# A transformer block with adaptive LayerNorm: normalisations on GpSimd in another form, x of the first chunk earlier, a shorter warm-up and a new order of work

## The chip, the cores and the metric

The kernel runs on one NeuronCore of a Trainium2 chip. The metric is the device time of one execution in microseconds (us); the kernel before takes 338.66 us, the median of three runs between 338.33 and 340.01. The five engines have separate instruction streams: PE is TensorE (matrix products; PEld is its weight load), DVE is VectorE, ACT is ScalarE, POOL is GpSimd, and SP is SyncE, which here only issues transfers. Each works through its instructions in the order in which they were emitted, and waits at semaphores for the others.

## What is computed

One transformer block on a sequence of 2048 tokens with 640 features, batch 1. A modulation vector `silu(c) @ w_mod` gives six vectors of 640, which scale, shift and gate the two halves of the block. Attention has 32 heads of 20 features, each token looking at the 256 tokens up to itself; the MLP has 1536 hidden features. Cut to what matters:

```python
mod = (silu(c) @ w_mod).reshape(1, 6, 1, -1)        # sa, ca, ga, sb, cb, gb
h = layernorm(x) * (1 + ca) + sa
q, k, v = split(h @ wqkv)                           # 32 heads of 20
p = softmax(where(0 <= i - j < 256, q k^T / sqrt(20), -1e9))
x = x + ga * ((p v) @ wo)
h = layernorm(x) * (1 + cb) + sb
x = x + gb * ((sigmoid(h @ w_gate) * (h @ w_up)) @ w_down)
```

The function `layernorm` has no weights of its own: `(x - m) / sqrt(v + 1e-5)` over the 640 features. All inputs and the output are bf16.

## The kernel before

The sequence is cut into eight chunks of 256 tokens, each of two blocks of 128 tokens. For every chunk the kernel does the same work: load x, LayerNorm, transpose and modulate (tile hT), project to queries, keys and values, bring queries and keys into the layout QT and KT, compute scores in sets of 2048 columns (PSUM tile S), exp on ScalarE into the tile E, mask E on GpSimd, multiply by V, divide by the sums (the softmax's denominators come out of the same product), send the result through DRAM into the tile oT, multiply by wo, add x, second LayerNorm, transpose and modulate (h2T), MLP, add, store.

The order is not written out by hand. Every instruction is handed to a planner as an operation with the engines that may run it, an expected duration on each, the tiles that it reads and writes, a latency after its end (`lat`) and a priority. The method `schedule` then plays the program through: on each engine it takes, of the operations that could start first (within `PE_EPS` on TensorE), the one with the lowest priority number, and so fixes order, buffer slots and, where several engines may do the work, the engine. A table `PRI` adds a number to the priority of every kind of operation of every chunk. `emit` writes the instructions in that order, with the semaphore waits that follow from the tiles. Transfers have an expected share of the bandwidth (`work`) in the plan. So the table and the expected durations set what waits behind what on the chip, although they change no instruction.

What the change touches:

- **LayerNorm** (`ln_stats`, L731 on). VectorE computes statistics (L741, two halves of 320 for each block) and aggregates them (L743); GpSimd adds the epsilon (L746) and takes the power -1/2 (L748) for both blocks at once; then each block is normalised by a `tensor_scalar` over 128 x 640 (L751), which subtracts the mean and multiplies by the power, on VectorE or on GpSimd as the planner decides. The planner expects 0.44 us on VectorE and 0.95 us on GpSimd. Chunks 0 and 1 are then transposed on TensorE against an identity, and scaled and shifted on the way out of PSUM (L786, L787); chunks 2 to 7, and all second LayerNorms, are transposed by SyncE's DMA (L757) and modulated in place (L765 on ScalarE, L766 on VectorE or GpSimd).
- **Masks** (L932, L934). They stand in the same GpSimd stream as the normalisations, and the product of E and V waits for all masks of its sets.
- **The head.** ScalarE's queue issues c and the two x blocks of chunk 0; SyncE's queue begins with five pieces of w_mod (into the memory of wd), then wq and wk in halves, x of chunk 1, wv, the other parts of w_mod (into the memory of wu and hh), wo. VectorE makes c_col and siluc and then silubc, silu(c) copied 128 times (L630). TensorE runs 18 warm-up matmuls of 512 columns on zeros (`warm`, L639), and single filling ones (`fill`, L650) between the pieces of the modulation product (psA, written S<-silubc,wd), whose result is copied to mA (L729) and used at L786 and L787. Two filling matmuls follow the fourth transpose of chunk 0.
- **Bulk loads.** A bulk transfer waits until the one `DEEP` places before it has landed: three are under way at most.

Nearly all matrix products are emitted by one helper and carry line 658 (659 where the array is divided, for the scores and for the product with V), so they are told apart by their tiles: M<-wq,hT is a query projection, M<-h2T,wg the MLP's gate, M<-E,V the product with V.

Of the kernel before, what the change touches and what calls it, by code (L numbers as in the profile page):

```python
# [8 lines left out]
ALU = mybir.AluOpType  # L9
# [8 lines left out]
NDT = D // 128  # L18
# [376 lines left out]
def c_pe(n):  # L395
# [3 lines left out]
PE_EPS = 0.117  # L399
PRI = {  # L400
    "amodu2": 349.1, "amodu3": 69.8, "amodu4": -2, "amodu5": 20.4, "amodu6": 21.9, "amodu7": 33.4, "apow0": -17.1,
    "apow1": -0.2, "apow2": -233.1, "apow3": -9.4, "apow4": -4.7, "apow5": -39.6, "apow6": -201.2, "apow7": 26.9,
    "astats1": 2, "astats2": -137.3, "astats3": 147.7, "astats4": 52, "astats5": 202.7, "astats6": 112.2,
    "astats7": -8.8, "atr3": -6.2, "atr4": -3.2, "atr5": -194.6, "atr6": 10.3, "atr7": -24.5, "axh0": -203,
    "axh2": -66.7, "axh3": 71.6, "axh4": -24.4, "axh5": 33.9, "axh6": -20.5, "axh7": 9.8, "bmodu0": -166.8,
    "bmodu1": 13.9, "bmodu2": 1.5, "bmodu3": 15.4, "bmodu4": -1.8, "bmodu5": 93.1, "bmodu6": 3.4, "bmodu7": -1.2,
    "bpow0": 4.3, "bpow1": 150.8, "bpow2": -11.8, "bpow3": -188.6, "bpow4": -35, "bpow5": 41.6, "bpow6": -22.5,
    "bpow7": -15.1, "bstats0": 20.1, "bstats1": 21.9, "bstats2": 16.8, "bstats3": 14.9, "bstats4": 25.8,
    "bstats5": -84.4, "bstats6": 22.4, "bstats7": -22.6, "btr0": -39.2, "btr1": -39.3, "btr2": -8.5, "btr3": 35,
    "btr5": -82, "btr6": 4.1, "btr7": -2.4, "bxh0": 24.8, "bxh1": -260.1, "bxh2": -55.1, "bxh3": 34, "bxh4": 72.4,  # L410
    "bxh5": 103.8, "bxh6": 81, "bxh7": 17.1, "divide_0": -16.1, "divide_1": 34.3, "divide_2": -154.9,
    "divide_3": 6.6, "divide_4": 14.8, "divide_5": -19.9, "divide_6": -11.9, "divide_7": 6.6, "down0": -15.1,
    "down1": -21.3, "down2": -20, "down4": 0.4, "down5": 1.9, "down7": 60.2, "evqk0": 16.1, "evqk1": 334.5,
    "evqk2": 27.2, "evqk3": 339.9, "evqk4": -0.3, "evqk5": 4.1, "evqk6": -33, "evqk7": -0.3, "evqt0": -11.6,
    "evqt1": -8.4, "evv0": 41.8, "evv1": 235.3, "evv2": 2.5, "evv3": -5.5, "evv4": -16.9, "evv5": -108.2,
    "evv6": -60.1, "evv7": -59.5, "exp0": -116.1, "exp1": -16.2, "exp2": -46.3, "exp3": 5.9, "exp4": -147.4,
    "exp5": -3.4, "exp6": 1.1, "exp7": -126.7, "glu_0": -1.3, "glu_1": 0.5, "glu_2": 26.7, "glu_3": -19.5,
    "glu_4": -37, "glu_5": -3.6, "glu_6": 8.5, "glu_7": 4.2, "hTe0": -31.6, "hTe1": 34.3, "mask0": 136.2,
    "mask2": -61.4, "mask3": 78.7, "mask4": -36.4, "mask5": -30.5, "mask6": 3.2, "mask7": 94.8, "mlpg0": -25,
    "mlpg1": -24.5, "mlpg2": -24, "mlpu0": -25, "mlpu1": -24.5, "mlpu2": -24, "modb": -25.7, "modc": -22.2,  # L420
    "n_ow_0": -20.3, "n_ow_1": -41.5, "n_ow_2": 44.8, "n_ow_3": 103.9, "n_ow_4": -5.8, "n_ow_5": -19.8,
    "n_ow_6": -1.4, "n_ow_7": 33.8, "oT_0": 17.5, "oT_1": 32.5, "oT_2": 12.6, "oT_3": 76.6, "oT_4": -64.2,
    "oT_5": 13.2, "oT_6": 2.6, "oT_7": 49.3, "out": 7.2, "projk0": -33.4, "projk2": 26.4, "projk3": -3.9,
    "projk4": 15.6, "projk5": 1.5, "projk6": 7.4, "projk7": 4, "projq0": -114.6, "projq2": 45.3, "projq3": -8.2,
    "projq4": 6.1, "projq5": -4, "projq6": 8.5, "projq7": -7.9, "projv0": -43.1, "projv1": 8.7, "projv2": 224.6,
    "projv4": -6, "projv5": 2.7, "projv6": 16.2, "projv7": 10.7, "ptr0": -337.9, "ptr1": -256.9, "pv0": -37.3,
    "pv1": -290.4, "pv2": -37.9, "pv3": -37.1, "pv4": -28.1, "pv5": -70.8, "pv6": -10.1, "pv7": -9.1, "qkt2": 7.9,
    "qkt3": 6.7, "qkt4": 64.8, "qkt5": -12.3, "qkt6": -3.6, "qkt7": -4.9, "qtr0": -154.4, "qtr1": -20.9,
    "recip_1": -1.9, "recip_2": 23.6, "recip_3": -2.4, "recip_4": 28.1, "recip_5": -22.7, "recip_6": 2.1,
    "recip_7": -9.2, "res1_0": -0.2, "res1_1": 5, "res1_2": 55.2, "res1_3": 7.6, "res1_4": 13.1, "res1_5": -5.3,  # L430
    "res1_6": -6.4, "res1_7": 11.2, "res2_0": 6.2, "res2_1": -29.9, "res2_2": -5.9, "res2_3": 1.7, "res2_4": -3.1,
    "res2_5": 40.9, "res2_6": -17.8, "res2_7": 2.6, "score0": -287.1, "score1": -347.7, "score2": -20.2,
    "score3": 1.8, "score4": -13.1, "score5": -50.5, "score6": -2.7, "score7": 11.5, "tanh_0": 29, "tanh_1": 20.7,
    "tanh_2": 23.5, "tanh_3": 22.7, "tanh_4": 26.2, "tanh_6": -2.3, "tanh_7": -20.3, "tr1_0": 19.8, "tr1_1": 6.2,
    "tr1_2": -28.1, "tr1_3": 15.6, "tr1_4": 45.4, "tr1_5": -90.8, "tr1_6": -19.7, "tr1_7": 5.2, "tr2_0": 204.6,
    "tr2_1": 224.6, "tr2_2": -128.4, "tr2_3": 42, "tr2_4": 64.5, "tr2_5": 40.4, "tr2_6": 0.1, "tr2_7": 27.5,
# [745 lines left out]
```

The softmax here doesn't subtract the row's maximum and nothing guards it: scores larger than these inputs give would overflow.

## Time and profile before

| what | value |
|---|---|
| median of three runs | 338.66 us |
| span of the profiled run | 335.3 us |
| exp, ACT L924 | 90 x 1876 ns = 168.9 us |
| masks, POOL L932 and L934 | 174 in 144.5 us |
| power, POOL L748 | 16 x 745 ns |
| normalisation on POOL, L751 | 6 x 2516 ns |
| normalisation on VectorE, L751 | 26 x 664 ns |
| modulation on POOL, L766 | 9 x 621 ns (hT), 8 x 559 ns (h2T) |
| statistics, DVE L741 | 64 x 478 ns |

The duration is the time of one instruction on its engine; it says nothing of whether anyone waits for it. For that one needs the chain of work that ended last, the waits of TensorE, and the busy time of each engine stage by stage. In a line of the timeline the first number is the start, the second the time that the merged instructions took, and the bracket at its end gives how long the engine had been idle before it and what ended that.

### The profile page before, as it was taken

How to read it: one execution, taken by the hardware profiler on the slowest of the kernel's cores; microseconds unless marked ns; L12 is line 12 of the kernel's file. 1: busy time of each engine (PE TensorE's matmuls, PEld its weight loads, DVE VectorE, ACT ScalarE, POOL GpSimd, SP SyncE). 2: the span in 40 equal slices, each digit the busy share in tenths (PEclk: the TensorE clock that was granted, in tenths of full speed). 3: DMA queues.
4: the chain of work that ended last, by engine and by line, in shares of the span. 5: the costliest groups of instructions: out<-in, count | busy, mean ns of one | idle time of the engine just before them, and what ended most of it. 6: DMA issues, size and time to landing. Idle time of an engine off the chain costs nothing.

```text
span 335.3 us, 10119 instructions
## 1 busy us (share of the span) xinstructions
PE 326.0 (97%) x4146; PEld 232.6 (69%) x4146; DVE 222.1 (66%) x441; ACT 229.7 (68%) x220; POOL 183.5 (55%) x255
## 2 busy tenths in 40 slices
PE   8898998999999999999999999999999999999996
PEld 3665555666776677766678666776676788887885
DVE  4597786889898857267996476744768663733332
ACT  1597799769988498777899779997699532230120
POOL 4138999766869685646675557656586610100000
PEclk9999999999999999999999999999999999999999
DMA  7989999696970296026851426100140231101101
GB/s 264 376 267 306 302 289 166 138 174 106 270 175 20 78 156 112 22 64 143 122 110 39 88 78 140 46 2 22 64 94 24 61 96 44 23 18 41 41 0 39
DMA packets 71686, 38.72 MB, mean 115 GB/s; under 512 B 46682, under 2 KB 68442, under 8 KB 71642
## 3 DMA queue, kind: packets, MB, share of 16 engines
q1 hardware_dynamic: 71344, 37.76, 46.3%
q8 instruction: 32, 0.52, 0.7%
q10 hardware_dynamic: 298, 0.33, 0.3%
q14 instruction: 12, 0.10, 0.1%
HBM read 21.96 MB, written 5.24 MB: 81 GB/s over the span
## 4 chain that ended last, share of the span: by engine, by line
PE 82%; POOL 6%; DMA 6%; DVE 2%; issue 2%; ACT 1%; SPq 0%; ACTq 0%; POOLq 0%
PE M L658 68%; PE S L659 8%; PE M L659 6%; DMA x<-in_A_x_dram 3%; POOL E L934 2%; POOL E L932 2%; POOL x L751 1%; DMA wo<-in_A_wo_dram 1%; DMA hh<-in_w_mod_dram 1%; DVE x L751 1%; ACT E L924 1%; POOL st L748 0%; DVE st L741 0%; DVE x L1099 0%; DVE stg L813 0%
## 5 line engine op out<-in xcount | busy, mean ns | idle before, releaser
L924 ACT ACTIVATE E<-S 128x2048 bf16<-128x2048 f32 x90 | 168.9, 1876 | 30.6 <-PE S L659 28.2
L932 POOL TENSOR_SCALAR_AFFINE_SELECT E<-E 128x512 bf16<-128x512 bf16 (+2 forms) x90 | 75.9, 844 | 72.3 <-ACT E L924 68.4
L934 POOL TENSOR_SCALAR_AFFINE_SELECT E<-E 128x512 bf16<-128x512 bf16 (+1 forms) x84 | 68.6, 816 | 0.0
L658 PE MATMUL M<-h2T,wg 128*128 128x256 bf16 x480 | 63.6, 273 | 0.1
L658 PE MATMUL M<-h2T,wu 128*128 128x256 bf16 x480 | 63.1, 273 | 0.0
L1080 DVE SCALAR_TENSOR_TENSOR hh<-sig,M 128x512 bf16<-128x512 f32 x48 | 32.6, 680 | 46.1 <-PE M L658 30.8
L1078 ACT ACTIVATE sig<-M 128x512 f32<-128x512 f32 x48 | 28.5, 594 | 43.9 <-PE M L658 43.9
L658 PE MATMUL M<-wd,hh 128*128 128x320 bf16 (+2 forms) x396 | 55.6, 295 | 0.0
L658 PEld LDWEIGHTS M<-h2T,wg 128*128 128x128 bf16 x480 | 45.0, 98 | 9.6 <-issue 2.7
L658 PEld LDWEIGHTS M<-h2T,wu 128*128 128x128 bf16 x480 | 45.9, 98 | 7.4 <-issue 1.7
L658 PEld LDWEIGHTS M<-wd,hh 128*128 128x128 bf16 x396 | 37.0, 98 | 15.4 <-issue 1.7
L659 PE MATMUL S<-QT,KT 20*128 20x256 bf16 (+1 forms) x960 | 35.9, 245 | 0.4 <-DVE KT L813 0.4
L1099 DVE TENSOR_TENSOR x<-M,x 128x320 bf16<-128x320 f32 (+2 forms) x33 | 15.5, 477 | 22.4 <-PE M L658 22.4
L975 DVE STREAM_TRANSPOSE T<-M 128x512 f32<-128x512 f32 x32 | 21.2, 695 | 13.0 <-PE M L659 13.0
L741 DVE BATCH_NORM_STATS2 st<-x 128x6 f32<-128x320 bf16 x64 | 28.2, 478 | 2.3 <-DMA x<-in_A_x_dram 1.9
L659 PEld LDWEIGHTS S<-QT,KT 20*128 20x128 bf16 x960 | 14.1, 92 | 20.7 <-ACT E L924 16.9
L658 PE MATMUL M<-wk,hT 128*128 128x320 bf16 x160 | 25.9, 300 | 0.0
L658 PE MATMUL M<-wq,hT 128*128 128x320 bf16 x160 | 25.5, 299 | 0.1
L658 PE MATMUL M<-wv,hT 128*128 128x320 bf16 x160 | 25.1, 300 | 0.0
L659 PE MATMUL M<-E,V 128*32 128x256 bf16 (+1 forms) x960 | 22.7, 246 | 2.2 <-POOL E L934 1.5
L658 PE MATMUL M<-wo,oT 128*128 128x320 bf16 x160 | 24.7, 300 | 0.0
L659 PEld LDWEIGHTS M<-E,V 128*32 128x32 bf16 x960 | 20.0, 97 | 6.5 <-POOL E L934 2.7
(76 smaller groups left out, 322.3 us busy)
## 6 DMA issues: line engine op xcount, KB each, us to landing
x<-in_A_x_dram SPq DMA_DIRECT2D x30, 160.0 KB
doc<-On SPq DMA_DIRECT2D x64, 40.0 KB
out_dram<-x SPq DMA_DIRECT2D x15, 160.0 KB
wg<-in_B_w_gate_dram SPq DMA_DIRECT2D x5, 384.0 KB
wu<-in_B_w_up_dram SPq DMA_DIRECT2D x5, 384.0 KB
wd<-in_B_w_down_dram SPq DMA_DIRECT2D x4, 480.0 KB
wd<-in_w_mod_dram SPq DMA_DIRECT2D x5, 320.0 KB
wu<-in_w_mod_dram SPq DMA_DIRECT2D x5, 320.0 KB
```

The costliest lines, as they stand in the source:

```text
L658: return e.matmul(o, l, r, start=st, stop=sp, skip_group_check=True)
L659: return e.matmul(o, l, r, start=st, stop=sp, tile_position=tp, skip_group_check=True)
L741: A("dve", lambda e, g, bi=bi, j=j: e.bn_stats(v(bi * 12 + j * 6, 6), src[bi].ap[:, j * 320:(j + 1) * 320]), 0.48, reads=[src[bi].r()], wr ...
L751: A(XHE, lambda e, g, bi=bi: e.tensor_scalar(dst[bi].ap[:], src[bi].ap[:], v(24 + 2 * bi, 1), v(30 + bi, 1), op0=ALU.subtract, op1=ALU.mul ...
L924: A("act", lambda e, eng: e.activation(E.ap[:], Sp.ap[:], ACT.Exp, scale=SM_SCALE), 1.876, reads=[Sp.r()], writes=[E.r()], prio=3, tag=f"e ...
L932: return e.affine_select(ap, ap, pattern=[[0, ap.shape[1]], [1, 128]], compare_op=ALU.is_ge, fill=0.0, base=0, channel_multiplier=-1)
L934: return e.affine_select(ap, ap, pattern=[[0, ap.shape[1]], [-1, 128]], compare_op=ALU.is_ge, fill=0.0, base=-1, channel_multiplier=1)
L975: A("dve", lambda e, g, h=h: e.transpose(T1.ap[:, 512 * h:512 * h + 512], X[h].ap), 0.694, reads=[X[h].r()], writes=[T1.r(h)], prio=3.5, t ...
L1078: A("act", lambda e, g, pg=pg, sg=sg: e.activation(sg.ap[:], pg.ap[:], ACT.Tanh, scale=0.5), c_act(512), reads=[pg.r()], writes=[sg.r()], ...
L1080: A("dve", lambda e, g, pu=pu, sg=sg, f0=f0: e.scalar_tensor_tensor(out=hh.ap[:, f0:f0 + 2, :], in0=sg.ap[:].rearrange("p (a b) -> p a b", ...
L1099: A("dve", lambda e, g, ps=ps, bi=bi, c0=c0, n=n: e.tensor_tensor(x1[bi].ap[:, c0:c0 + n], ps.ap[:, 0:n], x1[bi].ap[:, c0:c0 + n], op=ALU. ...
```

## The change

The normalisation gets another form wherever GpSimd is among the engines allowed: (x - m) r becomes x r + n with n = -m r. GpSimd computes n for each block as a product over one column, after the power. Thirty-two such products are new; they use two more columns of the statistics tile. The planner's durations for the normalisation become 0.5 us on VectorE and 1.2 us on GpSimd.

The two x blocks of chunk 0 move from ScalarE's queue, behind c, to the front of SyncE's queue. The warm-up falls from nine operations of two matmuls to five, and the filling ones between the pieces of the modulation grow from one matmul to two. The copy silubc is made in two halves: the first 64 columns, which the modulation of chunk 0 and the other column products need, and the rest, which only the gates need.

The planner is fed with other landing times of transfers (a `lat` of its own for x, w_mod, the weights and the transposes) and slightly other durations, allows four bulk transfers in place of three, and has a new table of priorities. The new table replaces every number, so it is left out here: with it the order of work changes on all engines, over the whole program.

```diff
-PE_EPS = 0.117
+PE_EPS = 0.141
 PRI = {
...
-DEEP = 3
+DEEP = 4
...
-PACE0 = -95.83
-PACE = 0.103
+PACE0 = 80.17
+PACE = -6.665
...
-FILL = 1
+FILL = 2
...
-        dma(lambda: t.ap[:], lambda: x_flat[b * 128:(b + 1) * 128, :], 0.47 if b > 1 else 0.9, writes=[t.r()], prio=prio, tmin=tmin, tag=f"x{b}" if pool is p_x0 else f"y{b}",
-            eng=eng, lat=0.05 if b > 1 else 1.2)
+        dma(lambda: t.ap[:], lambda: x_flat[b * 128:(b + 1) * 128, :], 0.47, writes=[t.r()], prio=prio, tmin=tmin, tag=f"x{b}" if pool is p_x0 else f"y{b}",
+            eng=eng, lat=-0.7 if b > 3 else -0.4 if b < 2 else -1.0)
...
-    x0[0], x0[1] = load_x(p_x0, 0, 0, eng="act"), load_x(p_x0, 1, 0, eng="act")
+    x0[0], x0[1] = load_x(p_x0, 0, 0), load_x(p_x0, 1, 0.1)
...
-    A("dve", lambda e, g: e.tensor_copy(silubc[:], siluc[:].unsqueeze(2).to_broadcast([128, NDT, 128])), 0.8,
-      reads=[R_siluc], writes=[R_silubc], prio=0)
+    A("dve", lambda e, g: e.tensor_copy(silubc[:, :, 0:MW], siluc[:].unsqueeze(2).to_broadcast([128, NDT, MW])), 0.45,
+      reads=[R_siluc], writes=[R_silubc], prio=-1)
+    R_silub2 = R("silub2")
+    A("dve", lambda e, g: e.tensor_copy(silubc[:, :, MW:128], siluc[:].unsqueeze(2).to_broadcast([128, NDT, 128 - MW])), 0.45,
+      reads=[R_siluc], writes=[R_silub2], prio=6)
...
-    for i in range(9):
+    for i in range(5):
...
-            A(XHE, lambda e, g, bi=bi: e.tensor_scalar(dst[bi].ap[:], src[bi].ap[:], v(24 + 2 * bi, 1), v(30 + bi, 1),
-                                                       op0=ALU.subtract, op1=ALU.mult), {"dve": 0.44, "pool": 0.95}, port=True,
-              reads=[src[bi].r(), st.r("r"), st.r(("m", bi))], writes=[dst[bi].r()], prio=prio - 0.5, tag=f"{ln}xh{a}")
+            if "pool" in XHE:
+                A("pool", lambda e, g, bi=bi: e.tensor_scalar(st.ap[:, 32 + bi:33 + bi], v(24 + 2 * bi, 1), v(30 + bi, 1), -1.0,
+                                                              op0=ALU.mult, op1=ALU.mult), 0.25,
+                  reads=[st.r("r"), st.r(("m", bi))], writes=[st.r(("n", bi))], prio=1, tag=f"{ln}pow{a}")
+
+                def xh(e, g, bi=bi):
+                    return e.tensor_scalar(dst[bi].ap[:], src[bi].ap[:], v(30 + bi, 1), v(32 + bi, 1), op0=ALU.mult, op1=ALU.add)
...
-                fills.append(fill(2 * FILL, [o]))
+                fills.append(fill(FILL, [o]))
```

In the changed kernel the lines stand some nine to thirteen lower: the normalisation is L760, the new product L755, the masks L945 and L947, the modulations L778 and L779, the matrix products L661 and L662, the warm-up L642 and the filling L653.

## The prediction

> **What bounds the kernel now.** I read the busy table first, then the chain of work that ended last, then the busy time by stage, then TensorE's waits, and last the timeline around the two longest of them.
>
> ```profile
> PE 326.0 (97%) x4146; PEld 232.6 (69%) x4146; DVE 222.1 (66%) x441; ACT 229.7 (68%) x220; POOL 183.5 (55%) x255
> ...
> PE 82%; POOL 6%; DMA 6%; DVE 2%; issue 2%; ACT 1%; SPq 0%; ACTq 0%; POOLq 0%
> ```
>
> TensorE is busy 97% and carries 82% of the chain; no other engine passes 69%. The end can move only by TensorE getting less work or fewer gaps, so the question is where the gaps are. Busy time by stage (from : to, length, then PE, PEld, DVE, ACT, POOL):
>
> ```profile
> 0.00:12.00 12.00, 9.81 (x87) 4.68 (x88) 5.96 (x18) 2.40 (x4) 4.56 (x28) 1.00 0.89 293
> 12.00:32.00 20.00, 18.57 (x227) 12.46 (x225) 15.46 (x40) 16.67 (x22) 8.97 (x9) 1.00 0.91 305
> 32.00:47.00 15.00, 14.12 (x188) 8.85 (x184) 12.19 (x25) 12.73 (x17) 14.73 (x18) 1.00 1.06 328
> 47.00:58.00 11.00, 9.57 (x124) 5.81 (x122) 8.32 (x15) 10.57 (x11) 11.00 (x11) 1.00 1.08 171
> 58.00:90.00 32.00, 31.97 (x437) 21.93 (x438) 26.93 (x58) 27.16 (x27) 23.40 (x34) 1.00 0.78 163
> 90.00:112.00 22.00, 21.41 (x272) 14.71 (x270) 20.26 (x40) 17.20 (x16) 18.41 (x21) 1.00 0.44 109
> 112.00:268.00 156.00, 155.85 (x2237) 110.20 (x2241) 104.90 (x197) 129.66 (x104) 99.81 (x134) 1.00 0.38 78
> 268.00:335.30 67.30, 64.75 (x600) 53.99 (x588) 28.10 (x52) 13.31 (x23) 2.58 (x5) 1.00 0.13 38
> ```
>
> From 112 to 268 TensorE lacks 0.15 us; from 268 it runs 600 matmuls of the last chunks and then 2.55 us pass in the last addition and store, which no edit touches. What can be won lies before 112 us: 2.19 us of gaps up to 12, and from 12 to 112 1.43 + 0.88 + 1.43 + 0.03 + 0.59 = 4.36 us. The head holds more than its gaps: until the first projection at 11.90 most of what TensorE runs is warm-up and filling (24 of the 512-column matmuls), useless in itself.
>
> The longest wait between 12 and 112, and what POOL did before it:
>
> ```profile
> 47.50 5.00 POOL L751 TENSOR_SCALAR x<-x,st 128x640 bf16<-128x640 bf16 x2
> 52.45 1.09 POOL L934 TENSOR_SCALAR_AFFINE_SELECT E<-E 128x1024 bf16<-128x1024 bf16 x1
> ...
> 58.03 0.40 PE L659 MATMUL M<-E,V 128*32 128x256 bf16 x8 [1.46 <-POOL E L934]
> ```
>
> POOL is busy in all 11 us of the stage 47 to 58. Two normalisations (L751) hold it for 5.00 us, a mask that belongs to the next product of E and V starts only at 52.45, and TensorE loses 1.46 us at 58.03. The head, where the LayerNorm of chunk 0 ends last:
>
> ```profile
> 7.62 0.89 DVE L741 BATCH_NORM_STATS2 st<-x 128x6 f32<-128x320 bf16 x2 [1.35 <-DMA x<-in_A_x_dram]
> ...
> 10.77 0.62 PE L658 MATMUL M<-ident,x 128*128 128x128 bf16 x8 [0.89 <-DVE x L751]
> ...
> 11.90 0.43 PE L658 MATMUL M<-wq,hT 128*128 128x320 bf16 x2
> ```
>
> **What the Trainium skill says.** "GPSIMD Engine Reference", section 3.1, gives some 1.8 cycles an element at 1.2 GHz for the tightest loop on GpSimd and more for others, beside a cost of dispatch. The trace fits for a product and a sum: 559 ns for 256 elements (L766 on h2T), of which 384 ns would be the loop. The subtraction and product of L751 does not fit: 2516 ns for 640, 4.7 cycles an element. "SBUF — State Buffer", section Who interferes with whom, says VectorE's two-port instructions and GpSimd exclude each other; the same L751 on VectorE takes from 439 to 1215 ns here, which agrees. "TensorE: Matmul & The Clock Gate", section What's actually happening, has half the clock until about 3.4 us of work: four 512-column matmuls take 1.89 us at 3.50 and 1.03 us at 5.53, so here it rose about 4 us after the first matmul at 1.30. "DMA: Bandwidth & Descriptors", section Issuing engines are not separate DMA queues, says all issuers share 16 engines; their share is 0.91 to 1.14 in every microsecond from 2 to 12.
>
> **The change, part by part.**
>
> *Product and sum on GpSimd.* Six normalisations on POOL become ten, 26 on VectorE become 22 (counted in the order each kernel emits). One takes, by the rows of L766, between 253 + (559 - 253)/254 x 638 = 1020 ns (fixed part from the 2-element row of L746) and 621 x 2.5 = 1550 ns; I take 1200. Against that stand 32 new products on one column, in front of every normalisation wherever it runs; the trace has none, its bounds are 102 ns (a memset of 4 columns) and 253 ns (L746), I take 200. The scheduler also puts 11 instead of 17 modulations on POOL. Sum: -6 x 2.52 - 17 x 0.59 + 10 x 1.2 + 11 x 0.59 + 32 x 0.2 = -0.2 us. So POOL's total hardly moves (-2 to +5 us with both ends), and at 55% a few microseconds cost nothing by themselves. What counts is the longest hold: 5.0 us of masks queued behind two normalisations becomes about 1.2 for one. In the new order the first two of the ten stand apart, and 23 masks and modulations then follow without one, where the old pair at 47.5 stood. I count the 1.46 us as won. The new products lengthen each LayerNorm by 0.4 us; behind that wait the DMA transposes of hT and h2T on SyncE, and their modulations; TensorE waits for none of these after 12 us now, so the slack there hides 0.4. Only chunk 0 has nothing ahead of it.
>
> *x of chunk 0 first on SyncE.* By the bytes per microsecond, 32 KB have moved at 2.0 and 276 KB at 3.0; x is 328 KB, so its blocks come at about 3.0 and 3.5 instead of up to 7.6. The five pieces of w_mod behind it are not later by this: x and w_mod together are 1.97 MB, and 2.08 MB have moved by 8.0 in either order. But VectorE now takes three statistics (0.45 each) and an aggregate (0.21) before c_col, so the column of silu(c) comes later: 3.0 + 1.8 + 0.25 = 5.05 for c_col, and from there about 1.05 us (1.46 from 3.61 to 5.07 before, less 0.41 for the half of the copy), 6.1 to 6.4 against 5.07. The LayerNorm of chunk 0 is done at about 7.9 (aggregate 5.4, then 0.25 + 0.72 + 2 x 0.2 and two normalisations of 0.4, with hops), no longer last. Now the modulation ends last. Its pieces stood 0.51 us apart (8.41, 8.92, 9.43) with one filling matmul of 0.21 between; with two that is 0.73: pieces at 6.3, 7.0, 7.8, 8.5, the transposes and a filling at 9.2, the fifth piece at 10.1 to 10.4. Then hop 0.2, copy 0.16, hop 0.1, and the 0.81 from hT's start at 11.09 to 11.90: first projection at 11.65, 0.25 us earlier. Bounds: the DMA alone would allow 9.3 (all bytes at 7.7), and x landing 1 us later than I think gives 12.6.
>
> *Shorter warm-up.* Ten instead of 18 warm-up matmuls and ten instead of six fillings. All eight that go lie ahead of 8.2 us, where TensorE waits for data, so their work is worth nothing; the ten left run from 1.3 to about 5.9, long enough for the clock to rise as before, and the fillings keep gaps below 1 us. Cost 0.
>
> *Order and landing times.* TensorE's matmuls are the same apart from the four; changes between its three tile modes fall from 201 to 199, at about 0.12 us each (a score set takes 0.33 us in the chain for 0.21 of columns): -0.2. SyncE may have four bulk loads under way instead of three. In the bytes, 20 to 24 us and 28 to 32 us show 234 and 242 GB/s beside 378 between; deeper queues should fill these. The modulation of the MLP waits for its last piece of w_mod at 30.28 (0.8 us of idle TensorE). The new order wants that piece at about 29, so the wait stays or shrinks: I take -0.4. The rest of the gaps from 12 to 112 (4.36 - 1.46 - 0.8 = 2.1 us: evictions of the first two chunks that a matmul waits for, wd's scaling, the 0.5 at 112) is what a new order can fill with other work; I take half, -1.0, and as much as 0.3 back for new gaps that no trace shows.
>
> **Sum.** -1.46 - 0.25 - 0.2 - 0.4 - 1.0 + 0.3 = -3.0; 338.66 - 3.0 = 335.7 us.
>
> **The rivals.** *B, all early gaps close:* 4.36 less 0.4 left, the head 1.5 nearer its DMA bound, 0.2 of modes: -5.7, 333.0. For it: POOL and SyncE cease to hold TensorE. Against: DMA share is near 1 up to 48 us, so bytes order the first third. *C, the gap changes its name:* TensorE reaches the later work sooner and waits there for w_mod, an eviction or an exp (ACT 10.57 of 11 us between 47 and 58); only -0.2 from modes and -0.2 elsewhere: 338.3. For it: ACT is as full as POOL there. Against: from 112 to 268 ACT, 83% busy, never holds TensorE. *D, slower:* silu's column at 7 or later puts the first projection at 12.6 (+0.7), and the 35 matmuls on the last part of w_mod, which the new order runs almost in one piece, wait 2 us for it; with 32 new products at 253 ns ahead of masks, another 0.3 remains: 338.66 + 3.0 - 0.6 (a part of the 1.46 still won) = 341.1. Against it: the old order ran the same weights at the same place with pieces between, and waited only 0.8 us.
>
> **How the numbers follow.** My forecast 0.53, B 0.19, C 0.16, D 0.12. The time is the forecast's, 335.7. The range leaves out D (0.12) and the far edge of B: from 332.8 to 339.0, C inside. Under 336.97 counts as faster: B, and nearly all of the forecast, 0.71. Within 0.5%: C and the slow edge of the forecast, 0.17. Slower: 0.12.
>
> **What would show it.** L760 on POOL near 1.2 us (right between 1.0 and 1.55), ten times; no wait of TensorE on a mask over 0.5 us before 60 us; the first wq matmul at 11.4 to 11.9, with the copy of mA behind the transposes; the fifth w_mod piece on TensorE about 10.2; 64 us without a gap at the end as before. I am wrong if L760 stays at 2.5 us, if wq starts past 12.3, if gaps from 12 to 112 still sum to over 4 us, or if ACT starts to hold TensorE after 112.

## The result, and the profile after

| kernel | median | ratio to the kernel before, 95% interval |
|---|---|---|
| before | 338.89 us (338.33 to 340.01) | |
| after | 343.80 us (343.16 to 344.87) | 1.0144 [1.0105, 1.0182] |

The change makes the kernel slower by 4.9 us, where 3.0 us less were forecast. A median below can hold a few executions that took over 1.5% longer than the shortest of the same kernel; the ratios leave those out, so the text argues from ratios (0.1% is 0.34 us). The profiled execution of before has a span of 335.3 us, and that of after, the longest of its four, 343.1, so the traces differ by 7.8 us, some 3 more than the medians.

Read in the same order as before. Busy time of the engines, and the shares of the chain that ended last, from the page of after:

```profile
PE 328.2 (96%) x4142; PEld 232.3 (68%) x4142; DVE 220.6 (64%) x440; ACT 232.2 (68%) x224; POOL 185.4 (54%) x285
...
PE 75%; DVE 9%; DMA 5%; SPq 3%; issue 2%; ACT 2%; POOL 2%; DVEq 0%; ACTq 0%
```

No engine's busy time moved by more than 2.5 us, and TensorE is as full. What changed is the chain: TensorE's share falls from 82% to 75%, VectorE's rises from 2% to 9% (a q marks the queue or sequencer of an engine). GpSimd, whose holds the change was to shorten, falls from 6% to 2%. So most of GpSimd's share of the chain went, and VectorE's took its place. By stage (from : to, length, then PE, PEld, DVE, ACT and POOL busy, the granted TensorE clock, the DMA share, GB/s):

```profile
0.00:12.00 12.00, 9.36 (x81) 4.05 (x81) 5.29 (x19) 2.03 (x4) 5.10 (x30) 1.00 0.85 264
12.00:32.00 20.00, 18.83 (x211) 13.40 (x212) 13.96 (x36) 16.56 (x28) 6.16 (x12) 1.00 1.01 344
32.00:47.00 15.00, 12.24 (x157) 7.32 (x155) 12.53 (x26) 8.94 (x11) 11.18 (x14) 0.89 0.90 296
47.00:58.00 11.00, 10.67 (x140) 6.51 (x133) 10.46 (x18) 9.54 (x11) 5.44 (x7) 1.00 0.30 62
58.00:90.00 32.00, 29.27 (x408) 18.50 (x405) 26.07 (x57) 27.42 (x28) 23.89 (x36) 1.00 0.88 166
90.00:112.00 22.00, 19.45 (x262) 14.64 (x260) 19.55 (x36) 16.06 (x15) 13.51 (x18) 1.00 0.62 160
112.00:268.00 156.00, 155.52 (x2151) 108.70 (x2152) 95.52 (x181) 129.72 (x108) 108.02 (x153) 1.00 0.35 71
```

What TensorE lacks in each stage, against before: up to 12 us 2.64 (was 2.19), then 1.17 (1.43), 2.76 (0.88), 0.33 (1.43), 2.73 (0.03), 2.55 (0.59), and from 112 to 268 0.48 (0.15). The stages from 12 to 112 lack 9.54 us in sum instead of 4.36. Two stages got better: 12 to 32 by a little, and 47 to 58, the one that the prediction had singled out. Three got worse, by 1.9 to 2.7 us. And in the stage 32 to 47 a number appears that was 1.00 throughout before: a mean clock of 0.89 over 15 us. It comes from 3.4 us at half clock, worth 1.7 us of full-speed work. The added idle time up to 268 us (6.0) and this make 7.7 of the 7.8 us between the traces.

The list of TensorE's waits names what stands there now (total, times, longest):

```profile
PE M L661 <- DVE stg L826: 2.9, 2, 2.7
PE M L661 <- DVE hh L1093: 1.9, 1, 1.9
PE S L662 <- ACT E L937: 1.5, 4, 0.7
...
PE M L661 <- DMA wv<-in_A_wqkv_dram: 0.9, 1, 0.9
PE M L662 <- POOL E L947: 0.9, 1, 0.9
```

Two single waits on VectorE head it. (The wait on a mask stands at 83.8 us. The one for wv, at 18.6 us, is not in the list of before: wv is issued at 11.40 us here and at 10.18 there.) The timeline around the first, about 36 us:

```profile
34.44 0.35 DVE L779 TENSOR_SCALAR hT<-hT,mA 128x256 bf16<-128x256 bf16 x1
...
35.09 4.35 POOL L945 TENSOR_SCALAR_AFFINE_SELECT E<-E 128x2048 bf16<-128x2048 bf16 x3
35.33 1.85 DVE L779 TENSOR_SCALAR hT<-hT,mA 128x256 bf16<-128x256 bf16 x1
...
37.10 1.39 DVE L1136 TENSOR_TENSOR wo<-wo,gbc 128x640 bf16<-128x640 bf16 x1
38.41 0.48 DVE L826 CAST stg<-M 128x320 bf16<-128x320 f32 x1
...
38.94 0.40 PE L661 MATMUL M<-ident,stg 128*128 128x128 bf16 x4 [2.67 <-DVE stg L826]
```

Read it from the bottom. The matmul waits 2.67 us for a copy of 0.48 us. That copy is third in VectorE's queue; in front of it are a modulation that takes 1.85 us where the one before it, at 34.44, took 0.35, and a scaling of wo that takes 1.39 where two at 32.75 took 1.02 together. Both run beside masks on GpSimd that began just before them. The Trainium skill describes this under "SBUF — State Buffer", section Who interferes with whom: VectorE's two-port instructions are kept out for the whole length of a GpSimd instruction that came first, and one with two inputs in SBUF contends with a GpSimd instruction that reads SBUF, as a mask does. The durations agree: the modulation ends 2.1 us after the mask's start, and a single mask of this size takes 2.00 us (at 42.19).

Right behind the gap, in windows of 2 us of the same trace:

```profile
38.00:40.00 2.00, 0.97 (x22) 0.56 (x22) 2.00 (x5) 0.60 (x1) 1.44 (x2) 1.00 1.05 375
40.00:42.00 2.00, 2.00 (x24) 1.09 (x13) 1.52 (x4) 1.75 (x1) 0.00 (x0) 0.55 1.05 411
42.00:44.00 2.00, 2.00 (x11) 1.16 (x10) 1.57 (x5) 0.36 (x2) 1.81 (x1) 0.59 0.86 318
44.00:46.00 2.00, 2.00 (x43) 1.40 (x41) 1.14 (x4) 0.64 (x2) 1.50 (x5) 1.00 0.48 166
```

TensorE counts as busy for all of 40 to 44, but at about half the clock: 18 matmuls of V take 4.29 us. A busy share doesn't show this; the clock column does. The second long wait, near 101 us, is the same queueing on VectorE:

```profile
88.45 2.40 SPq L536 DMA_DIRECT2D wd<-in_B_w_down_dram  x4
...
92.37 0.51 DVE L1077 TENSOR_TENSOR wd<-wd,gbc 128x640 bf16<-128x640 bf16 x1
...
95.26 7.04 DVE L1077 TENSOR_TENSOR wd<-wd,gbc 128x640 bf16<-128x640 bf16 x9 [0.84 <-DMA wd<-in_B_w_down_dram]
102.23 0.68 DVE L1093 SCALAR_TENSOR_TENSOR hh<-sig,M 128x512 bf16<-128x512 f32 x1
...
102.96 1.27 PE L661 MATMUL M<-h2T,wg 128*128 128x256 bf16 x10 [1.87 <-DVE hh L1093]
```

In the new order w_down is fetched in one go at 88 us, nine of its scalings run in a row, and the MLP's product hh, which frees the PSUM that TensorE needs, stands behind them. The same hold lengthens the row: the scaling at 92.37 takes 0.51 us, those of the row that start beside a mask between 0.74 and 1.37, and so the nine take 7.04.

### The profile page after: what moved, and what is told of

It is laid out like the page before. It is cut to its first block, busy times and chain, and to the rows that moved or that the text cites. A ratio compares the mean times of both kernels' runs of the same rounds, so it can differ in the third digit from the quotient of the medians.

```text
span 343.1 us, 10138 instructions
## 1 busy us (share of the span) xinstructions
PE 328.2 (96%) x4142; PEld 232.3 (68%) x4142; DVE 220.6 (64%) x440; ACT 232.2 (68%) x224; POOL 185.4 (54%) x285
## 4 chain that ended last, share of the span: by engine, by line
PE 75%; DVE 9%; DMA 5%; SPq 3%; issue 2%; ACT 2%; POOL 2%; DVEq 0%; ACTq 0%
PE M L661 62%; PE S L662 7%; PE M L662 6%; SPq L536 3%; ACT E L937 2%; DMA wv<-in_A_wqkv_dram 2%; DVE wd L1077 2%; DMA wd<-in_B_w_down_dram 2%; DVE hT L779 2%; DMA hT<-x 1%; DVE x L1051 1%; DVE st L744 1%; POOL E L945 1%; POOL E L947 1%; DVE Tn L995 1%
## 5 line engine op out<-in xcount | busy, mean ns | idle before, releaser
L945 POOL TENSOR_SCALAR_AFFINE_SELECT E<-E 128x512 bf16<-128x512 bf16 (+2 forms) x90 | 78.8, 877 | 79.5 <-ACT E L937 78.1
L947 POOL TENSOR_SCALAR_AFFINE_SELECT E<-E 128x512 bf16<-128x512 bf16 (+1 forms) x84 | 68.1, 812 | 0.0
L661 PE MATMUL M<-h2T,wg 128*128 128x256 bf16 x480 | 62.7, 273 | 2.0 <-DVE hh L1093 1.9
L661 PE MATMUL M<-h2T,wu 128*128 128x256 bf16 x480 | 64.4, 273 | 0.0
L661 PE MATMUL M<-wd,hh 128*128 128x320 bf16 (+2 forms) x396 | 56.1, 295 | 0.0
L661 PEld LDWEIGHTS M<-h2T,wg 128*128 128x128 bf16 x480 | 45.3, 98 | 10.9 <-issue 2.2
L661 PEld LDWEIGHTS M<-h2T,wu 128*128 128x128 bf16 x480 | 45.2, 98 | 8.6 <-issue 2.7
L661 PEld LDWEIGHTS M<-wd,hh 128*128 128x128 bf16 x396 | 37.0, 98 | 15.2 <-issue 1.5
L662 PE MATMUL S<-QT,KT 20*128 20x256 bf16 (+1 forms) x960 | 35.9, 245 | 1.6 <-ACT E L937 1.5
L749 POOL TENSOR_SCALAR st<-st 128x2 f32<-128x2 f32 x16 | 4.8, 304 | 47.0 <-DVE st L746 46.4
L662 PEld LDWEIGHTS S<-QT,KT 20*128 20x128 bf16 x960 | 14.1, 92 | 22.3 <-ACT E L937 18.1
L661 PE MATMUL M<-wv,hT 128*128 128x320 bf16 x160 | 27.1, 314 | 1.2 <-DMA wv<-in_A_wqkv_dram 0.9
L661 PE MATMUL M<-wq,hT 128*128 128x320 bf16 x160 | 24.7, 299 | 0.6 <-DVE V L826 0.3
L661 PE MATMUL M<-wo,oT 128*128 128x320 bf16 x160 | 24.6, 300 | 0.5 <-DVE x L1051 0.5
L661 PE MATMUL M<-wk,hT 128*128 128x320 bf16 x160 | 24.8, 300 | 0.1
L662 PE MATMUL M<-E,V 128*32 128x256 bf16 (+1 forms) x960 | 22.7, 246 | 1.5 <-POOL E L947 0.9
```

Of the source, the lines that this page charges most:

```text
L661: return e.matmul(o, l, r, start=st, stop=sp, skip_group_check=True)
L662: return e.matmul(o, l, r, start=st, stop=sp, tile_position=tp, skip_group_check=True)
L945: return e.affine_select(ap, ap, pattern=[[0, ap.shape[1]], [1, 128]], compare_op=ALU.is_ge, fill=0.0, base=0, channel_multiplier=-1)
L947: return e.affine_select(ap, ap, pattern=[[0, ap.shape[1]], [-1, 128]], compare_op=ALU.is_ge, fill=0.0, base=-1, channel_multiplier=1)
```

## The experiments

The theories named in the expectations: **O**, the written order costs the time and the three edits of instructions don't, mostly where a VectorE operation that TensorE needs stands behind others that are held beside GpSimd's masks; **P**, one of the edits costs it; **L**, the transfers make everything late, so that the next gap opens where one is closed; **S**, SyncE's issue time of x in front makes the loads late; **H**, the head, put back, wins its time again. In all of them the order of every engine is frozen as the kernel before or after has it; `ahead(engine, a, b)` then moves one operation of an engine just in front of another.

### The parts alone, in the order of before

b_form: only the form of the normalisation and its 32 products.

```diff
-    e.tensor_scalar(dst, src, mean, power, op0=ALU.subtract, op1=ALU.mult)
+    e.tensor_scalar(dst, src, power, neg, op0=ALU.mult, op1=ALU.add)
+    P.order["pool"].insert(P.order["pool"].index(power_op) + 1 + bi, neg_op)   # neg = mean * power * -1, one column
```

> The kernel before, its order on every engine as it was, with the product-and-sum normalisation and the 32 new one-column products on GpSimd behind each power. Theory O (the new order costs the time, the parts do not): the normalisation on GpSimd takes 0.87 us instead of 2.5, the wait of 1.46 us at 58 goes, 336.5 to 338 us, that is 0.5 to 0.8% under before. Theory P (a part costs it): the 32 products at 0.27 us hold masks and LayerNorms, 340 us or more.

Measured: 1.0002 [0.9972, 1.0033], no change. b_xfirst: only x of chunk 0 at the front of SyncE's queue.

```diff
+    for k, tag in enumerate(("x0", "x1")):      # out of ScalarE's queue, to the front of SyncE's
+        o = nth("act", tag, 0)
+        P.order["act"].remove(o)
+        o.eng = "sp"
+        P.order["sp"].insert(k, o)
```

> The kernel before in its own order, with only the two x blocks of chunk 0 moved from ScalarE's queue to the front of SyncE's. Theory S (SyncE issues back to back up to 10 us, so 0.9 us of two more issues at its front makes every later load 0.7 to 1 us late, and up to 48 us the kernel waits on loads): 339.5 to 340.3 us, 0.2 to 0.4% slower, with the wait for the last part of w_mod at 30 us longer than 0.8. Theory H (the head gains because x lands at 3.1 and 3.5): 338.2 to 338.7.

Measured: 1.0012 [0.9977, 1.0047]. b_warm: only four of the nine warm-up operations left out.

```diff
+    gone = [o for o in P.order["pe"] if o.tag == "warm"][4:8]
+    P.order["pe"] = [o for o in P.order["pe"] if o not in gone]
```

> The kernel before with four of its nine warm-up operations left out and nothing else changed. If the shorter warm-up costs nothing: 338.5 to 339.3 us, the first projection at the same time and the clock at full speed. If it costs (a colder TensorE clock in the head): the first projection's matmuls take longer before 16 us and the time is 340 us or more.

Measured: 1.0024 [0.9999, 1.0048]. Each part alone can't be told from nothing. b_all joins the three in the order of before.

> The kernel before in its own order, with all three parts at once: the new form, x of chunk 0 first on SyncE's queue, four of nine warm-up operations taken out. Theory O: 335.5 to 337.5 us, faster than before by the wait on masks and some tenths in the head. Theory P: 341 us or more, like the changed kernel, since it has the same parts.

Measured: 1.0042 [1.0017, 1.0067], a small loss of 1.4 us. Its profiled execution, 1.2 us above the median, shows one place where it can come from, in the waits from 20 to 35 us and in two windows:

```profile
PE M L658 <- DMA hh<-in_w_mod_dram: 2.4, 1, 2.4
```
```profile
28.00:30.00 2.00, 0.00 (x0) 0.00 (x0) 0.62 (x2) 0.56 (x1) 0.00 (x0) 1.00 0.40 118
30.00:32.00 2.00, 1.88 (x12) 1.16 (x12) 1.78 (x7) 0.44 (x1) 1.05 (x2) 0.50 0.70 196
```

TensorE comes to the last part of w_mod before it has landed, stands still for over 2 us, and then runs at half clock. Up to 8 us this kernel has moved 225 GB/s x 8 us = 1800 KB, against 260 x 8 = 2080 KB in before (b_form 265, b_xfirst 219, after 221). So x in front does slow the first loads: that much of theory S is right. But the wait for the last part of w_mod, which S expected to grow, is 0.7 us in b_xfirst against 0.8 in before, and no price could be seen; why it is 2.4 us in b_all is not shown. In the order of before the three parts together cost 0.4%, where the whole change costs 1.4%.

### The order alone

a_old: the order of after, with the parts taken out (old form, no products, x back on ScalarE's queue, the silu column ahead of the statistics). The shorter warm-up, the filling matmuls and the copy silubc in two halves stay.

```diff
-    e.tensor_scalar(dst, src, power, neg, op0=ALU.mult, op1=ALU.add)
+    e.tensor_scalar(dst, src, mean, power, op0=ALU.subtract, op1=ALU.mult)
+    P.order["pool"] = [o for o in P.order["pool"] if o not in negs]
+    P.order["act"].insert(k + 1, o)             # x0, x1 back behind c
```

> The order of the changed kernel alone: the form of the normalisation on GpSimd back to a difference and a product, the 32 negative products left out, x of chunk 0 back on ScalarE's queue with the first statistics behind the silu column. Only the written order and the five warm-up operations of the changed kernel stay. Theory O (the order costs the time, the parts do not): 343 us or more, with a gap of over 2 us between 33 and 39 us. Rival P (a part of the change costs it): 340 us or less, no such gap.

Measured: 1.0184 [1.0125, 1.0243]. The new order without the three parts is at least as slow as the whole change. One thing besides the order may weigh here: ten normalisations stand on GpSimd in the new order, and in the old form they take 25.2 us (10 x 2522 ns), against 8.7 in after. Its trace has the same collision 2 us earlier, followed by half a clock (0.50 from 38 to 40 us):

```profile
33.23 4.35 POOL L950 TENSOR_SCALAR_AFFINE_SELECT E<-E 128x2048 bf16<-128x2048 bf16 x3
...
34.02 1.30 DVE L784 TENSOR_SCALAR hT<-hT,mA 128x256 bf16<-128x256 bf16 x1
...
35.23 1.39 DVE L1141 TENSOR_TENSOR wo<-wo,gbc 128x640 bf16<-128x640 bf16 x1
36.55 0.48 DVE L831 CAST stg<-M 128x320 bf16<-128x320 f32 x1
...
37.08 0.61 PE L661 MATMUL M<-ident,stg 128*128 128x128 bf16 x4 [2.12 <-DVE stg L831]
```

Together with b_all, where the parts cost 0.4% in the order of before, this speaks for O and against P.

### The gap at 36 us

a_swap puts the copy that TensorE waits for in front of the two slow operations; a_both also puts the product hh of 102 us in front of seven scalings of w_down.

```diff
+    ahead("dve", nth("dve", "evqk1", 3), nth("dve", "amodu3", 1))   # both: copy before modulation and wo scaling
+    ahead("dve", nth("dve", "glu_0", 2), nth("dve", "wds", 5))      # a_both only: hh before seven scalings
```

> The changed kernel with one move in VectorE's stream: the copy of keys to stg that TensorE waits for at 38.9 goes ahead of the modulation of hT and the scaling of wo that stand before it. Theory O, in the form that a modulation blocked by a GpSimd mask holds the copy, and that the gap of 2.67 us then halves the clock for 3.4 us: the gap and the slow matmuls go, 339.0 to 340.5 us (about -4). Theory L (the gaps only show that everything is late, by transfers; close one and the next opens): 342.5 to 344 us. Theory P: no difference, 343.8.

> The same move, and a second one: the MLP's product hh that TensorE waits for at 102.96 goes ahead of seven of the ten scalings of wd that stand in a row before it on VectorE. Theory O: 1.9 us and up to 0.7 more beside the first move, 336.5 to 338.5 us. Theory L: at most 0.5 us less than with the first move alone. Theory P: 343.8.

Measured: 1.0154 [1.0117, 1.0191] and 1.0117 [1.0075, 1.0159]. Nothing is won by the first move. Its waits from 30 to 45 us say why:

```profile
PE M L661 <- DVE gbc L709: 2.1, 1, 2.1
```

The next operation in VectorE's queue that TensorE needs, a copy that frees another PSUM buffer, is still behind the same two. The gap has changed its name and the half clock stays. In a_both the wait for hh is gone; the 1.2 us between the two ratios is about that wait, though the intervals overlap.

a_order2 takes the cause away instead: the scaling of wo goes in front of the first modulation, before the mask starts, and the second modulation behind both copies.

```diff
+    ahead("dve", nth("dve", "wos", 4), nth("dve", "amodu3", 0))
+    ahead("dve", nth("dve", "amodu3", 1), nth("dve", "axh2", 0))
```

> The changed kernel with VectorE's order altered at one place: the last scaling of wo goes ahead of the first modulation of hT of chunk 3, and the second of these modulations goes behind the two copies to gbc. In the run with one copy moved, TensorE's gap only went from that copy to the copies to gbc behind the same two instructions; here nothing that TensorE waits for is left behind them. Theory O: no gap over 1 us between 34 and 42, no half clock, 339.5 to 340.5 us. Theory L: 342.5 or more.

Measured: 1.0066 [1.0042, 1.0089]. The stage 32 to 47 of its trace:

```profile
32.00:47.00 15.00, 12.33 (x170) 7.73 (x167) 11.68 (x29) 10.45 (x13) 11.12 (x14) 1.00 0.98 294
```

No gap from 34 to 40 us is over 0.8 us, the clock is 1.00 throughout, and 0.8% of the time, over half of the loss, is gone: 2.6 us, where theory O expected 3.3 to 4.3. A new gap of 1.5 us opens at 42.5, for a copy to V that stands on VectorE behind statistics whose x landed late (VectorE had waited 1.68 us for it). a_split reaches the same by the other side: VectorE's order stays, but GpSimd's mask of 2048 elements becomes four of 512.

```diff
+    if a == 0 and stride == 1:
+        for j in range(4):
+            ap = E.ap[:, j, :].rearrange("p (t c) -> p t c", c=128)
+            ins = e.affine_select(ap, ap, pattern=[[0, 4], [1, 128]], compare_op=ALU.is_ge, fill=0.0,
+                                  base=0, channel_multiplier=-1)
+        return ins
```

> The changed kernel with the masks of chunk 0 that have 2,048 elements per partition made as four masks of 512 each, same result, same order. Theory O (VectorE's instruction is held for one GpSimd mask at a time): the modulation that took 1.85 us beside the 2-us mask ends within about 1.0 us, TensorE's gap near 36-39 us shrinks below 1.2 us, no half clock follows at 40-44 us, and the time is 340.5 to 341.5 us; four instructions instead of one add at most some 0.3 us of GpSimd each. Rival (VectorE is held for as long as GpSimd has masks in its queue): the gap stays at 2.5 us or more and the time within 1 us of the changed kernel's 343.8 us.

Measured: 1.0067 [1.0046, 1.0088]. The timeline at the same place, and the stage:

```profile
35.51 2.65 POOL L946 TENSOR_SCALAR_AFFINE_SELECT E<-E 128x512 bf16<-128x512 bf16 x4
35.52 0.71 DVE L779 TENSOR_SCALAR hT<-hT,mA 128x256 bf16<-128x256 bf16 x1
...
36.15 0.93 DVE L1142 TENSOR_TENSOR wo<-wo,gbc 128x640 bf16<-128x640 bf16 x1
37.00 0.48 DVE L826 CAST stg<-M 128x320 bf16<-128x320 f32 x1
...
37.53 0.40 PE L661 MATMUL M<-ident,stg 128*128 128x128 bf16 x4 [1.07 <-DVE stg L826]
```
```profile
32.00:47.00 15.00, 13.28 (x203) 8.54 (x201) 12.82 (x31) 11.38 (x13) 12.32 (x21) 1.00 0.94 298
```

The modulation takes 0.71 us instead of 1.85 and the scaling 0.93 instead of 1.39: VectorE is held for one GpSimd instruction, not for as long as masks are queued. TensorE waits 1.07 us instead of 2.67, and the clock from 32 to 47 us is 1.00. Two edits on two engines thus give the same 0.8%. The control, b_split, makes the same split in the kernel before:

> The kernel before with the masks of chunk 0 of 2,048 elements per partition made as four of 512, same result and order. Theory O: in the order of before no VectorE operation that TensorE waits for lies beside these masks, so the split gives nothing: 338.5 to 339.5 us, and the gaps between 34 and 44 us stay below 0.6 us. Rival (the split by itself is worth the 2.7 us that it gave in the changed kernel, whatever the order): 337 us or less.

Measured: 1.0012 [0.9980, 1.0045]. In the order of before the split can't be told from nothing. The first collision is shown as a cause, and the half clock behind it comes with the gap. The mean granted clock of the timed executions says the same without a trace: one stretch of 3.4 us at half clock (1.7 of some 340 us) takes it from 1.000 to 0.995. All four executions of after and all six of a_swap are at 0.995 or below; 16 of a_order2's 22 and 17 of a_split's 22 are at 1.000, as are 130 of 166 of before.

### The other half

a_head undoes the head within after.

```diff
+    P.order["act"].insert(k + 1, o)                                 # x0, x1 back behind c
+    for o in [nth("dve", "", k) for k in (4, 5, 6, 7)]:             # c_col, siluc and silubc
+        ahead("dve", o, nth("dve", "astats0", 0))
+    ahead("pe", nth("pe", "modA", 5), nth("pe", "ptr0", 0))
```

> The changed kernel with x of chunk 0 back on ScalarE's queue behind c; for that the chain to silu's copy goes ahead of chunk 0's statistics on VectorE, and the fifth piece of the modulation ahead of chunk 0's transposes on TensorE. All else as in the changed kernel. Theory S: loads about 0.9 us earlier, first projection at 11.9, 342.5 to 343.2 us. Theory H: 344 us or more. If the gap at 36 to 39 us shrinks with earlier loads (theory L): 340 to 341.

Measured: 1.0131 [1.0097, 1.0164]: no gain to be told from after. The loads are early again (266 GB/s up to 8 us), and the gap before 38.2 us still costs 2.1 us, so late loads are not what opens it. But the edit does not bring the old head back in full: the transposes wait 1.8 us for the normalised x, and the first query projection starts only at 13.00 us (before 11.90, after 12.17). What the head by itself costs stays open. a_all3 joins this head, a_order2's moves and the move of hh.

> The changed kernel with the head of a_head, the order of a_order2, and the MLP's product hh ahead of seven scalings of wd. If the three causes add up (theory O with S): 343.8 - 0.9 - 3.8 - 1.8 = 337.3, between 336.5 and 338.5 us. Theory L: 341 or more.

Measured: 1.0111 [1.0066, 1.0156], no better than a_order2 alone. With the head shifted, the same mask caught another modulation at 34.14 us (2.03 us long), TensorE stood for 2.05 us and half a clock followed. So the repair holds only for the timing it was made for. a_fix leaves the head as in after and adds to a_order2 the move of hh, and moves the three residual sums of chunk 0 ahead of the modulations near 71 us. (The scalings of w_mod in its expectation are those of w_down.)

```diff
+    ahead("dve", nth("dve", "glu_0", 2), nth("dve", "wds", 5))
+    for k in range(3):
+        ahead("dve", nth("dve", "res1_0", k), nth("dve", "amodu4", 0))
```

> The changed kernel with three moves on VectorE: the last scaling of wo ahead of the two modulations near 35 us, the gated product near 102 us ahead of seven scalings of w_mod, and the three residual sums of chunk 0 ahead of the three modulations near 71 us. Theory O: the gaps add up; against the kernel with the first move alone (1.0066 of before) another 1.2 us goes with the second and 0.5 to 1 us with the third: 338.5 to 340 us. Theory L (everything is late by the transfers, so that the next gap opens where one is closed): 341.5 us or more.

Measured: 1.0111 [1.0065, 1.0157]; closing named gaps one by one did not add up. Its trace has a wait of 2.2 us for hh still, now before another product, and one of 1.5 us for a mask. a_splitall makes every mask in pieces of 512.

> The changed kernel with every mask of more than 512 elements per partition made in pieces of 512, in all chunks. The masks of chunk 0 alone gave 341.05 us. Theory O: the gaps at 70 to 73 us (2.2 us in sum), where three VectorE modulations lie beside masks of 1,024 elements, lose about a half, and the one near 82 us too: 339.5 to 340.5 us; GpSimd's added instructions (about 0.18 us each for some 60 masks) are hidden. Theory L: the gaps stay in sum, 340.8 us or more.

Measured: 1.0081 [1.0054, 1.0109], not better than a_split. After the first collision one half of theory L fits better than O: the next gap opens where one is closed. That the transfers are the reason is not shown; in a_head earlier loads won nothing. The rest, 0.7% or 2.3 us, is spread: a_split still lacks 1.70 us of TensorE from 58 to 90 us (before 0.03), in three gaps of 0.7, 0.7 and 0.9 us between 70 and 73 where the modulations of chunk 4, the exp and the residual sums meet, and its mean clock there is 0.95 in this execution. Half clock isn't the whole of it: the 17 executions of a_split at 1.000 take 341.0 us on the mean, those of before at 1.000, timed with them, 338.9. The cause of the rest stays open; three attempts at it failed.

### Where the forecast gain went

b_form removed the wait that the prediction counted, and showed another. First the load and the product in before, then b_form:

```profile
61.53 0.39 SPq L536 DMA_DIRECT2D oT<-doc  x1
...
65.80 2.48 PE L658 MATMUL M<-wo,oT 128*128 128x320 bf16 x17
```

```profile
57.47 1.50 PE L659 MATMUL M<-E,V 128*32 128x256 bf16 x64
...
59.52 3.62 SPq L761 DMA_TRANSPOSE hT<-x  x2
63.23 0.54 SPq L536 DMA_DIRECT2D x<-in_A_x_dram  x1
63.96 0.39 SPq L536 DMA_DIRECT2D oT<-doc  x1
...
66.72 0.57 PE L658 MATMUL M<-wo,oT 128*128 128x320 bf16 x3 [1.40 <-issue]
```

The product of E and V at 57.47 now starts without a wait; in before it waited 1.46 us for the mask. But 9 us later the product with wo stands still (idle 1.64 us by the starts of the matmuls), because the load of oT was issued only at 63.96, behind two transposes and a load of x on SyncE's queue; in before it was issued at 61.53. TensorE is 0.6 us earlier here, oT 2.4 us later. Two gaps before that had grown as well, at 36.4 us from 0.3 to 1.0 and at 43.8 from 0.6 to 0.9. b_ot1 is b_form with that load between the two transposes, b_ot0 with it in front of both.

```diff
+    ahead("sp", nth("sp", "oT_0", 1), nth("sp", "atr4", 1))         # b_ot0: nth("sp", "atr4", 0)
```

> The order of the kernel before with the new form of the normalisation and its 32 products, and one move on SyncE's queue: the load of oT that the 1.64-us gap at 65 us waits for is issued between the two transposes of chunk 4's x, not behind both. If that gap is a plain wait behind a 3.6-us stretch of issues, it shrinks to under 0.5 us and the time is 337.5 to 338.3 us, which beats both kernels by 0.2 to 0.4 per cent. Theory L (the next gap opens): another gap of 1 us or more appears between 66 and 85 us, and the time stays at 338.8 us or more.

> As the run before, but the load of oT ahead of both transposes of chunk 4's x. It should close the gap at 65 us too; the transposes then come some 2 us later, so that the modulation of chunk 4 may hold TensorE near 68 us: 337.5 to 339 us. If it is as good as the other place, the transposes had room; if it is worse by 1 us, they were next in line.

Measured: b_ot1 0.9975 [0.9957, 0.9994] (median 338.71 beside 339.31 for before), b_ot0 0.9995 [0.9968, 1.0022]. The profiled execution of b_ot1 is 3.7 us above its median and has 6.8 us of half clock from 39 us on, so only the place itself is read from it:

```profile
65.79 0.45 SPq L536 DMA_DIRECT2D oT<-doc  x1
66.30 2.14 SPq L761 DMA_TRANSPOSE hT<-x  x1
...
70.45 1.53 PE L658 MATMUL M<-wo,oT 128*128 128x320 bf16 x10
```

oT is now issued 4.7 us ahead of its product, instead of 2.8, and the product starts without a wait. In b_ot0 it starts without a wait too, but ten matmuls later TensorE waits 1.22 us for a copy on VectorE, so the place between the transposes may be the better one; the intervals overlap. b_ot1 beats both kernels of this study, a quarter of a per cent under before: 0.8 us of the 1.46, by its interval 0.2 to 1.5. The trace shows that the move closes the gap; that it makes the difference to b_form is likely but not shown, because these two intervals overlap as well.

## Why the prediction was wrong, point by point

- **Product and sum on GpSimd.** The mechanism was right. Ten on GpSimd, by shape: 868 ns, under the lower bound of 1020, which I had scaled from the modulation; the new products 271 ns, over the upper bound of 253; GpSimd's total +1.9 us, inside -2 to +5, though partly by luck: the normalisations came 3.3 us under what I took for them, and the masks, which I had left as they were, took 147.1 us instead of 144.4. (My terms as printed sum to -0.3, not -0.2.)

```profile
L760 POOL TENSOR_SCALAR x<-x,st 128x640 bf16<-128x640 bf16 x10 | 8.7, 868 | 0.2 <-POOL st L755 0.2
L755 POOL TENSOR_SCALAR st<-st 128x1 f32<-128x1 f32 x32 | 8.2, 271 | 1.6
```

- **"I count the 1.46 us as won."** The wait itself went, as said; no mask holds TensorE over 0.5 us before 60. But by itself the part gave nothing that could be measured (1.0002), and in b_form's trace the load of oT was due right behind. This is the idea of rival C, a gap that changes its name, though C had named other waits; the step failed by reading one wait and not the next one on the same path. The trace of before had it: oT was issued 4.3 us ahead of its product, b_form shows that 2.8 us with a wait at their end are used, so the slack was no more than some 1.5 us.
- **The head.** The step that failed is "the five pieces of w_mod behind it are not later by this". I took bytes moved as given; but in the new order SyncE issues x before w_mod, and 310 KB fewer have moved by 8 us. The pieces came at 6.04, 6.92, 7.70 and 9.09 us, the fourth after a wait of 0.50 for its transfer, the fifth at 10.70; the first query projection at 12.17, not 11.65. The silu column came a little earlier than forecast: c_col starts at 4.87 us, forecast for 5.05 (three statistics and an aggregate make 1.56 us at the prices given, not 1.8), and the first half of the copy is done at 5.85, forecast for 6.1 to 6.4. What this cost at the end is not shown: b_xfirst, x in front alone, is 1.0012 [0.9977, 1.0047].
- **Shorter warm-up, cost 0.** 1.0024 [0.9999, 1.0048]: not told from 0, and at most 1.6 us.
- **The wait for the last part of w_mod, -0.4.** It is gone from the list of after, as forecast, while a wait of 0.9 for wv is new. In the old order it is 0.8 in before, 0.7 in b_xfirst and 2.4 in b_all.
- **"I take half, -1.0, and as much as 0.3 back for new gaps."** This term sank the forecast: 0.3 us for new gaps was put down without a reason. Gaps from 12 to 112 should have come to 4.36 - 1.46 - 0.4 - 1.0 + 0.3 = 1.8 us and came to 9.54 in the trace of after, the two longest of them 2.67 and 1.87 us, both behind VectorE operations held beside masks. The first, with the half clock behind it, is worth 0.8% by a_order2 and by a_split, some 2.6 us. I had seen the lock between VectorE and GpSimd in the trace of before (L751 on VectorE from 439 to 1215 ns) and used it for nothing: the new order puts a modulation and a scaling beside the long masks of chunk 0, with the copies that TensorE needs behind them. The cause of the other new gaps stays open. The emitted orders of VectorE and GpSimd around the masks of chunk 0 would have shown it as possible, not as certain.
- **No term for the clock.** 1.7 us of the loss at 40 us is half clock after a gap. The prediction spoke of the clock only for the warm-up.
- **After 112 us.** As forecast: 0.48 us lacking, no wait on ScalarE of note.
- **The rivals.** D had the right side (341.1), for reasons that didn't hold: silu was not late and the wait for w_mod did not grow. Its chance of 0.12 left little room for an order in which every number of the table is new.

## What to carry to other kernels

When a new order replaces an old one in a tuned kernel, the idle time that it removes can be read from the old trace but what it adds can't; so look in the emitted order for short operations that the bottleneck engine waits for and that stand behind a VectorE operation beside a long GpSimd one, and give the risk a term of its own. A removed wait is worth its length only if the next thing on the same path has slack: read when the transfer for the following product was issued before counting it as won. Where VectorE must work beside masks and TensorE waits behind it, cutting the masks bounds the hold; cutting all the others too brought nothing more here.

## What the runs showed of the hardware that was not expected

- **A gap of some 2 us in the middle of the work can halve the clock for 3.4 us.** Over all 18 traces, from 14 us on and counted from matmul start to matmul start less the time of the columns, 11 of the 12 single gaps of TensorE of 2.05 us or more were followed by a stretch at half clock, and one (2.37 us, a_fix) was not; of 19 gaps from 1.3 to 2.03 us one was (1.87 us, a_splitall). In a_split, a_old and a_swap half clock also followed three gaps of 0.5 to 1.0 us within some 3 us; in after and a_both such a group was not followed by it. Each of these stretches took 3.41 us, twice that in b_ot1. "TensorE: Matmul & The Clock Gate", section What's actually happening, gives an idle window of about 3.4 us that runs freely; the length of the slow stretch fits that window, but here idle time well short of it was enough. So a gap of 2.3 us costs about 4.0, an estimate: 2.3 and half of 3.41.
- **The same normalisation costs GpSimd a third in the other form.** A difference and a product took 2516 ns for 640 elements, a product and a sum 868 ns, with both scalars from columns in each case; a_old, the old form in the new order, has 2522 ns. A lower cost was forecast, but not one this low.
